# An attention and GEGLU block on one core: q of the plain units given out sooner, sums of squares on TensorE, one more buffer for exponentials

## The chip, the cores and the metric

The kernel runs on one core of one Trainium2 chip. The metric is the device time of one execution in microseconds (us). Before the change it is 1726.62 us at the median of three runs.

## The reference

```python
h = layernorm(x) * (1 + ca) + sa                 # x: 2048 x 512; ca, sa, ... from silu(c) @ w_mod
q = h @ wq                                       # 32 heads of 128
p = softmax(q @ k.T * 128 ** -0.5)               # k, v: 8 heads, the last 512 keys of the cache
x = x + ga * ((p @ v) @ wo)
h = layernorm(x) * (1 + cb) + sb
x = x + gb * ((gelu(h @ w_gate) * (h @ w_up)) @ w_down)   # 1792 wide
```

All inputs and the output are float32.

## The kernel before

**Products.** Almost every float32 product is three float16 products of 512 columns, high x high and the two mixed terms; `mm3` issues them (line 91, whose rows in the profile carry the names of their tiles). This text calls such a triple a group. The operands are scaled so that the halves fit; each scale comes from a sum of squares of a weight tile. `sumsq` takes it: a Square on ScalarE with `accum_out` over a tile of 128x512 (line 220). Then `sums` adds over partitions by a product with ones (line 224, tile `pst`), and `norm2` takes the root on GpSimd.

**Units and slots.** The attention is cut into 128 units: one head, 512 query rows, 512 keys. Each unit is four slots of 128 query rows, so there are 512 slots. In slot t TensorE makes the scores (`scores`, one group, tile `ps`, two buffers), VectorE the maximum (`peak`, line 1000), ScalarE the exponential (`expo`, line 1009, tile `ee`); ScalarE writes the scaled high half of slot t-2 (`high`, line 1021), VectorE the low half of slot t-3 (`low`, line 1026), and SP then issues the transpose of that tile into `pt` (line 1030). After the scores, TensorE takes up to three groups from a queue `work`, and when that is empty from `ywork`; in slots 0 to 7 it takes 2, 2, 0, 0, 2, 2, 0, 0.

**What lies in the queue.** At the first slot of unit u, `pushes` appends the groups that belong there: four groups that make q of the next unit (tile `pq`), four groups of probabilities times V for unit u-2 (tile `po`), and from unit 10 on parts of the next q by a seven-product scheme (tiles `qa`, `qb`, `qc`). The first twelve units, of weight groups g = 0, 1 and 2, are "plain": their q come from `q_plain`, four groups each, with both halves of wq in two tiles `rw`. Products with wo (tile `py`, four groups for 128 rows) come in `ywork` in units 7 to 11, and later in `work`, one such tile in a unit. The order of instructions on every engine is that of the program.

**Loads.** `sched` gives each load positions: the first is the slot of its first use, and the load goes out up to three slots ahead, when the buffer's last step lies behind it. `sched_pair` loads the two wq tiles of a weight group into two buffers `rw` and runs the square of each, then `w_spread`, then the splitting into halves; for group 1 GpSimd does the splitting (lines 161, 162, 165). All loads and transposes stand in SP's one queue.

**Places of the exponentials.** `expo` writes to SBUF (tag "e", 6 buffers), and for the slots named in `PSE` to a bank of PSUM, of the ring "acc" (5 banks, shared with `pq`, `po`, `py` and `pst`) or to the bank "qa".

Of the kernel before, what the change touches and what calls it, by code (L numbers as in the profile page):

```python
# [10 lines left out]
F32 = mybir.dt.float32  # L11
# [39 lines left out]
NP16 = 4  # L51
NV16 = 2
NPT = 3
NE = 6
CB = (11, 27)
PSE = dict.fromkeys((5, 7, 8, 9, 14, 18, 19, 21, 22, 23, 25, 26, 27), "acc") | dict.fromkeys((11, 15, 20, 24, 28), "qa")
EARLY = (2, 2, 0, 0, 2, 2, 0, 0)
WOS = ((6, 7, 8, 9), (-9, -8, -6, -5), (-16, -15, -14, -13))
WOP = ((23, 24, 26, 27), (10, 12, 16, 17), (-6, -4, 10, 12), (-6, -4, -3, -2))
# [6 lines left out]
def block_kernel(ctx: ExitStack, tc: tile.TileContext, x, kT, v, wq, wo, wg, wu, wd, cT, wc, wm, out):  # L66
# [141 lines left out]
    def mod_scale(j, name, const_, m=None, mid=nop, box=None):  # L208
# [6 lines left out]
        ts(cols[:, j:j + 2, :], cols[:, j:j + 2, :], inv, TOP13 / RT)  # L215
        pool_ts(col(name), s, const_ * RT / TOP13)

    def sumsq(out, src):
        with nc.allow_low_precision(reason="only a scale follows from it, which the margin in norm2 covers"):
            nc.scalar.activation(junk, src, AF.Square, scale=PRE, accum_out=out)  # L220

# [343 lines left out]
        return load, norm, split, turn  # L565

    def turned_out(qb, dt):
        tag, n = (("qt", 3), ("v16", 2))[dt % 2]
        f = pool.tile([P, D], F32, tag=tag, name="hf", bufs=n)
        v = f.rearrange("p (t q) -> p t q", t=QT)  # L570
        sc = cols[:, 4, dt:dt + 1]
        nc.scalar.activation(v, TURN[qb][:, :, dt, :], AF.Identity, scale=sc, bias=cols[:, 3, dt:dt + 1])
        put_off(2, lambda: nc.vector.scalar_tensor_tensor(v, TURN[qb][:, :, KT + dt, :], sc, v, op0=ALU.mult, op1=ALU.add))
        put_off(4, lambda: dma(spilled(3, qb)[:, dt, :], f))
# [57 lines left out]
        return pair("v16", "v16", 2)  # L632

    def get_qt():
        return pair("qt", "qt", 3)

    def get_w(k):
        return pair(f"w{k}", f"w{k}", 2)
# [106 lines left out]
    def at(key, *fns):  # L745
        later.setdefault(key, []).extend(fns)
# [488 lines left out]
    for g in range(NG):  # L1235
        half, pr = divmod(g, NPR)
        t0 = 16 * g
        qd = pr // 2
        srcs = [wq[2 * pr], wq[2 * pr + 1]]
        by = col("wsc", pr)  # L1240
        spread = None if half else lambda m, pr=pr: w_spread(pr, m)
        if 0 < g < GW:
            a, b = plain_steps(g, by)
            sched_pair(g, srcs, t0 - (19 if g > 1 else 13), spread, [(t0 - (12 if g > 1 else 8), a)], [(t0 - (8 if g > 1 else 7), b)])
        elif g >= GW and (not half or pr < GW):
            sched_set(g, srcs, t0, by, spread)
            if not half:
                a, b, c, d, e, f = SETPOS2 if g == GW else SETPOS
                for k, pos in ((0, t0 - b + 4), (3, t0 - c + 4), (1, t0 - e + 4), (2, t0 - f + 4)):
                    at(pos, lambda g=g, k=k: store_set(g, k))  # L1250
        elif half:
            for k, hi in ((0, 15), (1, 10), (2, 9), (3, 7)):
                within(t0 - 18, t0 - hi, lambda g=g, pr=pr, k=k: set_fetch(g, pr, k))
        if half:
            within(t0 - 14, t0 - 5, lambda pr=pr: k_fetch(pr))
            if pr % 2 == 0:
                within(t0 - 6, t0 + 3, lambda qd=qd: v_fetch(qd))
                for k in range(4):
                    within(t0 + 4 + 2 * k, t0 + 22 + 2 * k, lambda h=4 * qd + k: wo_fetch(h))
        else:  # L1260
            if g > 0:
                if pr % 2 == 0:
                    load, stat, spread_, parts = k_items(pr)
                    sched(t0 - (22 if g > 2 else 20), (load, [stat]))
                    at(("w", t0 - (19 if g > 2 else 17)), spread_)
                load, stat, spread_, parts = k_items(pr)
                sched(t0 - (7 if g > 2 else 4 if g > 1 else 6), (load, [parts if g != 2 else lambda parts=parts: soon(parts(True))]))
                at(t0 - (3 if g > 2 else 1 if g > 1 else 2), lambda pr=pr: store(("k", pr), KV[0, pr, 0]))
                if pr % 2 == 0:
                    load, stat, spread_, parts = v_items(qd)  # L1270
                    sched(t0 + 1, (load, [stat, spread_, parts]), t0 + 3, t0 + (6 if g > 2 else 5))
                    at(t0 + 10, lambda qd=qd: store(("v", qd), KV[0, qd, 1]))
            if pr % 2 == 0:
                wo_items(qd, [t0 + o + (qd == 7) for o in WOS[min(qd, 2)]], [t0 + o for o in WOP[min(qd, 2) + qd // 6]])
# [276 lines left out]
    def pushes(u, y):  # L1551
        g, k = divmod(u, 4)
        pv = pv_tasks(u - 2) if 2 <= u < NU + 2 else []
        if u >= NU:
            if k == 0:
                f = items(g)
                return y + f[4] + f[5] + pv + f[3]
            if k == 1:
                f = items(g + 1)
                return f[1] + f[2] + pv + f[6]  # L1560
            return []
        nxt = items(g + 1) if g + 1 >= GW else None
        if g < GW:
            w = q_plain(u + 1) if 0 < u + 1 < 4 * GW else []
            if u + 1 == 4 * GW:
                return nxt[2] + nxt[6] + pv + nxt[7]
            return w + pv + (nxt[1] if nxt and k == 2 else [])
        f = items(g)
        if k == 0:
            return y[:3] + f[4] + y[3:] + pv  # L1570
        if k == 1:
            return f[5] + y + nxt[1] + pv
        if k == 2:
            return f[3] + nxt[2] + y + pv
        return nxt[6] + y + pv + nxt[7]

    ctx.enter_context(tc.manual_schedule(engines={mybir.EngineType.SP}))
    with tc.manual_schedule():
        begin()
        nexty, invs = [], {}  # L1580
        for t in range(T + TAIL):
            now[0] = t
            u, s = divmod(t, 4)
            if s == 0:
                y = nexty.pop(0) if nexty and GW * 4 <= u <= NU else []
                if u > 2 and u % 2 == 1 and u - 2 < NU:
                    nexty += push_y(u - 2)
                work += pushes(u, y)
            if s == 2 and (t >= T or u < GW * 4) and nexty:
                ywork += nexty.pop(0)  # L1590
                while t >= T and nexty:
                    ywork += nexty.pop(0)
            if t < T:
                scores(t)
            inv = invs.pop(t, nop)
            if t < T:
                peak(t)
            run(("e", t))
            inv()
            if 0 <= t - LLAG < T:  # L1600
                low(t - LLAG)
            run(("d", t))
            if t < T:
                expo(t)
                if t % 2:
                    invs[t + 1] = recips(t - 1)
            if 0 <= t - HLAG < T:
                high(t - HLAG)
            run(("x", t))
            if 4 <= t < 4 + KT:  # L1610
                gate_cols(t - 4)
            for _ in range(4 if t >= T else EARLY[t] if t < len(EARLY) else 3):
                pop()
            run(t)
            for q in pending.values():
                while q and q[0][0] <= t:
                    q.pop(0)[2]()
            run(("w", t))
            spare(t)
            moved[0] = 0  # L1620
            if t == T + 2:
                for k in range(1, len(hold), 2):
                    for step in zip(*hold[k:k + 2]):
                        for fn in step:
                            fn()
                hold.clear()
        while ywork or work or any(k[0] in "dex" for k in later if isinstance(k, tuple)):
            now[0] += 1
            run(("e", now[0]))
            run(("d", now[0]))  # L1630
            run(("x", now[0]))
            for _ in range(4):
                pop()
            run(now[0])
        run(now[0] + 1)
        run(now[0] + 2)
        run(now[0] + 3)
# [90 lines left out]
    def yt_turn(g, c, qb):  # L1728

        def split():  # L1730
            tag, bufs = (("qt", 3), ("v16", 2))[YR.get("n", 0) % 2]
            u = YR["u", c, qb] = pool.tile([P, 2, QB], U16, tag=tag, name="yu", bufs=bufs)
            nc.scalar.activation(u, YT[g, c, qb].bitcast(U16).rearrange("p (r h) -> p h r", h=2), AF.Copy)

        def turn():
            if ("t", qb) not in YR:
                YR["t", qb] = pool.tile([P, KT, 2 * QT, P], U16, tag="pt", name="yv", bufs=NPT)
            nc.sync.dma_start_transpose(YR["t", qb][:, c], YR.pop(("u", c, qb)).rearrange("p a b -> p (a b)"))

        split()  # L1740
        put_off(3, turn)
        YR["n"] = YR.get("n", 0) + 1
        if YR["n"] == 3 * QT:
            put_off(4, lambda: rows_in(g, 1, (("acc", 2 * QT),) * 2))
# [116 lines left out]
```

## Time and profile before

| what | value |
|---|---|
| median of three runs | 1726.62 us (1725.72 to 1727.48) |
| span of the profiled execution | 1724.3 us, first to last instruction |
| time around the span, against the median | 2.3 us |
| TensorE / VectorE / ScalarE / GpSimd busy | 1705.4 / 1424.2 / 1257.4 / 1088.1 us |
| granted TensorE clock, mean | 0.999 |
| DMA queue of SP | 341.30 MB, 85.3% of 16 engines |

The profiled execution is listed by its span; its own time lies within the runs' 1725.72 to 1727.48 us. Slot 0 begins at 23.11 us, slot 12 at 53.08, slot 28 at 88.06, slot 64 at 181.38. A row of the timeline gives start, length, engine, line, tile written and tiles read, and the count of merged instructions; what stands in brackets is the idle time ahead of it and what ended it. PE rows are products, PEld rows are loads of the stationary operand.

### The profile page before, as it was taken

The numbers are of one execution on the slowest core, as the hardware profiler recorded it, in microseconds if no ns is written. First come the engines' busy times: TensorE is split into PE (matmuls) and PEld (weight loads), VectorE is DVE, ScalarE is ACT, GpSimd is POOL, SyncE is SP. The second block draws the span as 40 slices with busy tenths as digits, with TensorE's granted clock in tenths as the row PEclk, the third lists the DMA queues.
The fourth block names the chain that finished last, engine by engine and source line by source line (L and its number), as shares of the span: only waits on it lengthen the run. The fifth ranks groups of instructions, "written<-read, shape, count | busy, mean of one in ns | idle before, by whom it ended". The sixth has DMA issues, their size and how long they took to land.

```text
span 1724.3 us, 26250 instructions
## 1 busy us (share of the span) xinstructions
PE 1705.4 (99%) x7961; PEld 780.0 (45%) x7961; DVE 1424.2 (83%) x2480; ACT 1257.4 (73%) x2823; POOL 1088.1 (63%) x1322
## 2 busy tenths in 40 slices
PE   7999999999999999999999999999999999999999
PEld 4344444444444444444444444444444444444444
DVE  8888888888888999888888888888896788676666
ACT  7988788888878877888778777788785354455442
POOL 3879777776788884655665755757760345735424
PEclk9999999999999999999999999999999999999999
DMA  7999999999999998999999999899997556365353
GB/s 242 222 207 214 214 217 205 226 202 227 213 217 236 201 212 181 212 211 225 216 220 222 211 227 206 198 236 212 222 232 162 164 144 195 121 165 174 99 158 102
DMA packets 693454, 343.51 MB, mean 199 GB/s; under 512 B 579136, under 2 KB 602688, under 8 KB 693312
## 3 DMA queue, kind: packets, MB, share of 16 engines
q1 hardware_dynamic: 693024, 341.30, 85.3%
q8 instruction: 63, 1.03, 0.3%
q14 instruction: 79, 0.65, 0.1%
q10 hardware_dynamic: 288, 0.52, 0.1%
HBM read 137.50 MB, written 63.70 MB: 117 GB/s over the span
## 4 chain that ended last, share of the span: by engine, by line
PE 92%; ACT 4%; DVE 2%; DMA 2%; issue 1%; SPq 0%; ACTq 0%; DVEq 0%
PE py L91 20%; PE po L91 18%; PE ps L91 17%; PE fa L91 8%; PE qa L91 8%; PE fc L91 4%; PE qc L91 4%; PE ya L91 4%; PE qb L91 2%; PE fb L91 2%; PE yc L91 2%; ACT ee L1009 1%; ACT p L1021 1%; PE yb L91 1%; DMA rw<-in_wq 1%
## 5 line engine op out<-in xcount | busy, mean ns | idle before, releaser
L1009 ACT ACTIVATE ee<-ps,nm 128x512 f32<-128x512 f32 x512 | 349.7, 683 | 185.3 <-DVE nm L1000 182.7
L1026 DVE SCALAR_TENSOR_TENSOR p<-ee,rr,p 128x512 f16<-128x512 f32 x512 | 454.4, 888 | 8.5 <-ACT p L1021 8.0
L1000 DVE TENSOR_REDUCE nm<-ps 128x1 f32<-128x512 f32 x512 | 350.1, 684 | 96.8 <-PE ps L91 94.9
L91 PE MATMUL ps<-k,qt 128*128 128x512 f16 x1536 | 414.7, 379 | 4.4 <-ACT ee L1009 3.3
L1021 ACT ACTIVATE p<-ee,rr 128x512 f16<-128x512 f32 x512 | 363.9, 711 | 16.5 <-DVE rr L1017 11.8
L91 PE MATMUL po<-pt,v 128*128 128x512 f16 x1536 | 372.9, 379 | 2.1 <-DMA pt<-p 0.8
L91 PE MATMUL py<-wo,ot 128*128 128x512 f16 x1536 | 371.3, 379 | 0.0
L91 PEld LDWEIGHTS <-w 128*128 128x128 f16 x2184 | 213.4, 98 | 259.6 <-issue 2.0
L91 PEld LDWEIGHTS <-v 128*128 128x128 f16 x1536 | 149.8, 98 | 184.6 <-issue 3.0
L91 PEld LDWEIGHTS <-ot 128*128 128x128 f16 x1536 | 150.3, 98 | 181.2
L91 PEld LDWEIGHTS <-qt 128*128 128x128 f16 x1536 | 145.7, 98 | 178.0 <-issue 6.0
L1337 POOL TENSOR_TENSOR fg<-fg 128x512 f32<-128x512 f32 x48 | 62.9, 1311 | 135.8 <-DVE fg L1311 133.0
L754 DVE SCALAR_TENSOR_TENSOR ot<-po,ot 128x512 f16<-128x512 f32 x128 | 87.8, 686 | 40.4 <-ACT ot L753 39.9
L1321 ACT ACTIVATE at<-fg 128x512 f16<-128x512 f32 x92 | 56.3, 626 | 77.8 <-DVE fg L1311 61.0
L1009 ACT ACTIVATION_READ_ACCUMULATOR ee<-ps,nm 128x1 f32 x512 | 100.1, 196 | 0.0
L970 DVE SCALAR_TENSOR_TENSOR acc<-py,ysc,acc 128x512 f32<-128x512 f32 x128 | 94.7, 739 | 5.3 <-PE py L91 5.3
L91 PE MATMUL qa<-t,w 128*128 128x512 f16 x348 | 84.9, 379 | 0.0
L91 PE MATMUL fa<-t,w 128*128 128x512 f16 x336 | 81.7, 379 | 0.1
L237 POOL TENSOR_TENSOR lw<-lw,half__86 128x1 f32<-128x1 f32 x38 | 25.9, 681 | 85.7 <-DVE lw L188 85.6
L753 ACT ACTIVATE ot<-po 128x512 f16<-128x512 f32 x128 | 73.9, 578 | 5.0 <-PE po L91 5.0
L404 POOL TENSOR_TENSOR rs<-rs,nhalf 128x1 f32<-128x1 f32 x32 | 18.5, 577 | 93.7 <-DVE rs L398 85.8
L91 PEld LDWEIGHTS <-wo 128*128 128x128 f16 x504 | 49.3, 98 | 59.7 <-issue 0.5
(258 smaller groups left out, 2802.9 us busy)
## 6 DMA issues: line engine op xcount, KB each, us to landing
w<-kept SPq DMA_DIRECT2D x123, 256.0 KB, 3.3
wo<-kept SPq DMA_DIRECT2D x72, 256.0 KB, 3.2
kept<-stage SPq DMA_DIRECT2D x67, 256.0 KB, 3.0
raw<-in_wo SPq DMA_DIRECT2D x56, 256.0 KB, 3.2
kept<-w SPq DMA_DIRECT2D x39, 256.0 KB, 3.0
rw<-in_wq SPq DMA_DIRECT2D x38, 256.0 KB, 3.1
hs<-hf SPq DMA_DIRECT2D x32, 256.0 KB, 2.9
pt<-p SPq DMA_TRANSPOSE x512, 3.4
```

The lines of the kernel that those rows point to most:

```text
L91: nc.tensor.matmul(ps, a, b, start=first and n == 0, stop=last and n == 2, skip_group_check=chain)
L237: nc.gpsimd.tensor_tensor(out, out, half_, op=ALU.pow)
L404: nc.gpsimd.tensor_tensor(st["rs"], st["rs"], nhalf, op=ALU.pow)
L753: nc.scalar.activation(t[:, 0, :], src, AF.Copy, scale=scale)
L754: return lambda: nc.vector.scalar_tensor_tensor(t[:, 1, :], src, scale, t[:, 0, :], op0=ALU.mult, op1=ALU.subtract)
L970: nc.vector.scalar_tensor_tensor(acc[ti], st["p"], by, acc[ti], op0=ALU.mult, op1=ALU.add)
L1000: nc.vector.tensor_reduce(nm, E[t]["ps"], axis=AX.X, op=ALU.max, negate=True)
L1009: nc.scalar.activation(e, E[t]["ps"], AF.Exp, bias=E[t]["nm"], scale=1.0, accum_out=sm[:, t % 2:t % 2 + 1])
L1021: nc.scalar.activation(p16[:, 0, :], E[t]["e"], AF.Copy, scale=E[t]["r"])
L1026: nc.vector.scalar_tensor_tensor(p16[:, 1, :], E[t]["e"], E[t]["r"], p16[:, 0, :], op0=ALU.mult, op1=ALU.subtract)
L1321: nc.scalar.activation(t[:, 0, :], g, AF.Copy)
L1337: nc.gpsimd.tensor_tensor(g[o], g[a], g[b], op=ALU.subtract)
```

## The change

Four things change.

- `sumsq` in slots 0 to 27 calls the new `gram`: four float32 products of a tile's 128x128 parts with themselves, summed in a bank of "acc", and one read of its diagonal on VectorE with `accum_out`. 13 squares fall there: wq of groups 1 and 2 (4), K of group 2 (1), wo (8).
- `pushes` hands out q of units 5 to 11 by the table `QAT`, up to two units sooner; the tiles `qt` have five buffers in place of three. In units 8 to 11 a second tile of products with wo is put into `ywork` at the unit's first slot.
- The loads and squares of wq of group 2 start three slots sooner, its splitting three and five; the square of K of group 2 three slots sooner.
- `NE` is 7, and eight exponentials (slots 5, 7, 8, 19, 21, 23, 25, 27) go to SBUF and no longer to "acc".

```diff
-NE = 6
+NE = 7
+NQT = 5
+QAT = ((1,), (2,), (3,), (4, 5), (6, 7), (8,), (9, 10), (11,))
+GRAM = 28
-PSE = dict.fromkeys((5, 7, 8, 9, 14, 18, 19, 21, 22, 23, 25, 26, 27), "acc") | ...
+PSE = dict.fromkeys((9, 14, 18, 22, 26), "acc") | ...
...
+    def gram(out, src):
+        ps = bank("acc", "gram", NACC)
+        for k in range(KT):
+            sl = slice(k * P, (k + 1) * P)
+            nc.tensor.matmul(ps[:, 0:P], src[:, sl], src[:, sl], start=k == 0, stop=k == KT - 1)
+        ...
+            nc.vector.scalar_tensor_tensor(small.tile([P, P], F32, tag="gd", name="gd", bufs=1), ps[:, 0:P], PRE * PRE, ident, op0=ALU.mult, op1=ALU.mult, accum_out=out)
+
     def sumsq(out, src):
+        if 0 <= now[0] < GRAM:
+            return gram(out, src)
...
-            sched_pair(g, srcs, t0 - (19 if g > 1 else 13), spread, [(t0 - (12 if g > 1 else 8), a)], [(t0 - (8 if g > 1 else 7), b)])
+            sched_pair(g, srcs, t0 - (22 if g > 1 else 13), spread, [(t0 - (15 if g > 1 else 8), a)], [(t0 - (13 if g > 1 else 7), b)])
...
-                    sched(t0 - (22 if g > 2 else 20), (load, [stat]))
-                    at(("w", t0 - (19 if g > 2 else 17)), spread_)
+                    sched(t0 - (22 if g > 2 else 23), (load, [stat]))
+                    at(("w", t0 - (19 if g > 2 else 20)), spread_)
...
-            w = q_plain(u + 1) if 0 < u + 1 < 4 * GW else []
+            w = [q_plain(n) for n in (QAT[u] if u < len(QAT) else ())]
...
-            return w + pv + (nxt[1] if nxt and k == 2 else [])
+            return (w[0] if w else []) + pv + (w[1] if len(w) > 1 else []) + (nxt[1] if nxt and k == 2 else [])
...
-            if s == 2 and (t >= T or u < GW * 4) and nexty:
+            if (s == 2 and (t >= T or u < GW * 4) or s == 0 and u in (8, 9, 10, 11)) and nexty:
```

What this does to the order of instructions is shown at three places.

First, TensorE at the end of slot 10 (`po` is probabilities times V, `ps` the scores, `qt` the q halves, `pq` the next q, `w_659` and `w_691` the split wq). Before, the last product with V and the scores of slots 11 and 12, then the first product of the next q:

```order
L91 MATMUL po<-pt,v_588 128x512
L91 LDWEIGHTS qt
L91 MATMUL ps<-k,qt 128x512
...
L91 LDWEIGHTS w_659
L91 MATMUL pq<-b_201,w_659 128x512
```

Now, at the same place:

```order
L94 MATMUL po<-pt,v_600 128x512
L225 MATMUL gram<-rw 128x128 x4
L94 LDWEIGHTS qt
L94 MATMUL ps<-k,qt 128x512
...
L225 MATMUL gram<-rw 128x128 x4
...
L94 LDWEIGHTS w_691
L94 MATMUL pq<-b_201,w_691 128x512
```

The products on the two wq tiles of group 2 stand ahead of the scores of slot 11 and of slot 12.

Second, SP's queue in slots 6 to 11. `p_...` are probabilities by slot: `p_585`, `p_621`, `p_644`, `p_675` and `p_711` before, and `p_597`, `p_641`, `p_670`, `p_707` and `p_757` now, are those of slots 4 to 8. Before:

```order
L97 DMA wor<-in_wo 128x512
L1030 DMA_TRANSPOSE pt<-p_585 128x8x128
L97 DMA raw<-in_kT 128x512
L1030 DMA_TRANSPOSE pt<-p_621 128x8x128
L1030 DMA_TRANSPOSE pt<-p_644 128x8x128
L97 DMA u_689<-hs_1_473 128x512
L97 DMA raw<-in_kT 128x512
L1030 DMA_TRANSPOSE pt<-p_675 128x8x128
L97 DMA cb<-hs_1_473 128x512
L97 DMA rw<-in_wq 128x512
L1030 DMA_TRANSPOSE pt<-p_711 128x8x128
L97 DMA rw<-in_wq 128x512
```

Now:

```order
L100 DMA wor<-in_wo 128x512
L100 DMA raw<-in_kT 128x512
L1043 DMA_TRANSPOSE pt<-p_597 128x8x128
L100 DMA raw<-in_kT 128x512
L1043 DMA_TRANSPOSE pt<-p_641 128x8x128
L1043 DMA_TRANSPOSE pt<-p_670 128x8x128
L100 DMA u_721<-hs_1_473 128x512
L100 DMA rw<-in_wq 128x512
L1043 DMA_TRANSPOSE pt<-p_707 128x8x128
L100 DMA cb<-hs_1_473 128x512
L100 DMA rw<-in_wq 128x512
L1043 DMA_TRANSPOSE pt<-p_757 128x8x128
```

Each load of `rw` moves up by one transpose, while its first reader moves up by three slots; the loads of K move up by one transpose as well.

Third, TensorE at slot 32 (`py` is the product with wo). Before, after the scores of that slot:

```order
L91 MATMUL py<-wo,ot 128x512
L91 LDWEIGHTS qt
L91 MATMUL ps<-k,qt 128x512
...
L91 LDWEIGHTS w_1118
L91 MATMUL pq<-b_201,w_1118 128x512
```

Now:

```order
L94 MATMUL py<-wo,ot 128x512
L94 LDWEIGHTS qt
L94 MATMUL ps<-k,qt 128x512
...
L94 LDWEIGHTS v_600
L94 MATMUL po<-pt,v_600 128x512
```

The two or three groups of q that stood between the scores and the product with V are gone from here and from slots 36 and 40; they now stand in slots 14 to 27. Counted in groups, slots 14, 15, 18, 19, 26 and 27 gain 12, and slots 51, 54, 55, 58, 59, 62 and 63, which held products with wo, lose 12 as those are used up earlier.

More of the change, by code (lines that the diff above doesn't have):

```diff
@@ L53 @@
 NPT = 3
-NE = 6
+NE = 7
+NQT = 5
+QAT = ((1,), (2,), (3,), (4, 5), (6, 7), (8,), (9, 10), (11,))
+GRAM = 28
 CB = (11, 27)
-PSE = dict.fromkeys((5, 7, 8, 9, 14, 18, 19, 21, 22, 23, 25, 26, 27), "acc") | dict.fromkeys((11, 15, 20, 24, 28), "qa")
+PSE = dict.fromkeys((9, 14, 18, 22, 26), "acc") | dict.fromkeys((11, 15, 20, 24, 28), "qa")
 EARLY = (2, 2, 0, 0, 2, 2, 0, 0)
@@ L216, in mod_scale @@
         pool_ts(col(name), s, const_ * RT / TOP13)
+    def gram(out, src):
[3 more added lines that the diff above has]
+            nc.tensor.matmul(ps[:, 0:P], src[:, sl], src[:, sl], start=k == 0, stop=k == KT - 1)
+        with nc.allow_low_precision(reason="only a scale follows from it, which the margin in norm2 covers"):
+            nc.vector.scalar_tensor_tensor(small.tile([P, P], F32, tag="gd", name="gd", bufs=1), ps[:, 0:P], PRE * PRE, ident, op0=ALU.mult, op1=ALU.mult, accum_out=out)
     def sumsq(out, src):
+        if 0 <= now[0] < GRAM:
+            return gram(out, src)
         with nc.allow_low_precision(reason="only a scale follows from it, which the margin in norm2 covers"):
@@ L567, in turned_out @@
     def turned_out(qb, dt):
-        tag, n = (("qt", 3), ("v16", 2))[dt % 2]
+        tag, n = (("qt", NQT), ("v16", 2))[dt % 2]
         f = pool.tile([P, D], F32, tag=tag, name="hf", bufs=n)
@@ L634, in get_qt @@
     def get_qt():
-        return pair("qt", "qt", 3)
+        return pair("qt", "qt", NQT)
     def get_w(k):
@@ L1730, in split @@
         def split():
-            tag, bufs = (("qt", 3), ("v16", 2))[YR.get("n", 0) % 2]
+            tag, bufs = (("qt", NQT), ("v16", 2))[YR.get("n", 0) % 2]
             u = YR["u", c, qb] = pool.tile([P, 2, QB], U16, tag=tag, name="yu", bufs=bufs)
```

## The prediction

> **What bounds the kernel now.** I read the page first, then the busy time by stage, then TensorE's timeline in the first 100 us, then the queue of transfers.
>
> ```profile
> span 1724.3 us, 26250 instructions
> ...
> PE 1705.4 (99%) x7961; PEld 780.0 (45%) x7961; DVE 1424.2 (83%) x2480; ACT 1257.4 (73%) x2823; POOL 1088.1 (63%) x1322
> ```
>
> The profiled span is 1724.3 us; the runs took 1725.72 to 1727.48, so some 2.3 us lie around it at the median of 1726.62. I make the sum against the span and add it to the median. A share of 99% for TensorE says nothing on single stages, so here are those the change touches: slots 3 to 11, 12 to 27, 28 to 31, 32 to 51 and 52 to 63 (their edges are starts of scores). Columns: length, then busy us of PE, PEld, DVE, ACT, POOL, then the granted clock.
>
> ```profile
> 33.13:53.08 19.95, 17.87 (x75) 7.62 (x73) 16.25 (x31) 18.75 (x47) 15.09 (x23) 1.00 0.97 230
> 53.08:88.06 34.98, 32.42 (x147) 13.88 (x147) 29.18 (x58) 32.86 (x80) 28.21 (x38) 1.00 1.07 220
> 88.06:99.64 11.58, 10.70 (x49) 4.62 (x49) 10.13 (x20) 11.19 (x29) 6.81 (x11) 1.00 0.97 186
> 99.64:151.54 51.90, 51.90 (x245) 23.60 (x244) 45.41 (x81) 41.89 (x99) 44.87 (x55) 1.00 0.95 213
> 151.54:181.38 29.84, 29.84 (x141) 13.54 (x140) 25.86 (x45) 24.71 (x58) 26.75 (x33) 1.00 1.05 223
> ```
>
> Up to about 97 us ScalarE sets the pace (94% busy in both of the first rows) and TensorE has gaps; from 99.64 on TensorE has none. A product's busy time includes a tail that overlaps the next one, so I count gaps by the pace from start to start:
>
> ```profile
> 88.90 2.10 PE L91 MATMUL pq<-b,w 128*128 128x512 f16 x9
> 90.84 0.81 PE L91 MATMUL ps<-k,qt 128*128 128x512 f16 x3
> ```
>
> Nine products take 1.94 us, 0.2156 each, and a group of three 0.647. Slots 3 to 11 hold 9 scores and 12 groups (63 products, 13.6 us) and four gate products (3.4, below): 17.0 of 19.95, so 2.9 us of gaps. Slots 12 to 27: 144 products, 31.0 of 34.98, 3.9 of gaps. Slots 28 to 31: 48 products, 10.4 of 11.58, 1.2. In all 8.0 us. Since TensorE is full from there on, the end moves by what is added to TensorE's work, less the gaps that vanish, plus new gaps. That is the whole sum.
>
> **The products that replace the squares.** 13 squares fall into slots 0 to 27 (4 of wq, 1 of K, 8 of wo). Each becomes four float32 products of 128x128x128. The nearest rows:
>
> ```profile
> 5.58 3.47 PE L1041 MATMUL mps<-silu,wct 128*128 128x1 f32 x16
> ...
> 31.72 1.58 PE L443 MATMUL pln<-ident,xb 128*128 128x128 f32 x13
> ...
> 34.45 1.02 PE L1181 MATMUL gps<-wmr,silu 128*128 128x512 f32 x2
> 35.31 1.57 PE L91 MATMUL pq<-y,w 128*128 128x512 f16 x6
> ```
>
> A gate product (one instruction, two rows) keeps TensorE 0.86 us for 512 columns, four times a float16 product. For 128 columns that is 0.215, per square 0.86, for 13 squares **+11.2**. The transposes, 0.12 each, would give 6.3; the one-column products of the cold start, 0.217 a row and two rows each, 22.6. I take 11.2: it is the same kind of product in the same stage. None of it is hidden, but for the gaps counted next.
>
> On ScalarE the squares go, 0.61 us each on the chain:
>
> ```profile
> 39.90 0.61 ACT junk L220 x2
> ```
>
> That is 7.9 us off the engine which bounds slots 3 to 27. After the change TensorE needs more than ScalarE there (slots 12 to 27: 31.0 + 4 x 0.86 + 12 moved groups x 0.647 = 42.2 us against ScalarE's 32.86), so the relief is worth the gaps alone: at most **-8.0**, I take **-7.2**, since some waits have other causes; the low end is -5. The eight exponentials that go to SBUF, the diagonal's read on VectorE (13 times, between nothing and the 0.69 us of a 512-column read below, so 0 to 9 us beside 45.4 busy in 54.9 us) and the seventh buffer cost nothing while TensorE is the longer; without that cover VectorE would be full.
>
> ```profile
> L754 DVE SCALAR_TENSOR_TENSOR ot<-po,ot 128x512 f16<-128x512 f32 x9 | 6.2, 688 | 0.8 <-ACT ot L753 0.7
> ```
>
> **The wait that the earlier statistics add.** The statistics of the second wq pair (unit group 2) move from slots 13 and 14 to 10 and 11. Their buffers are two, held by group 1 until GpSimd has split it, and the loads stand in SP's queue behind the transposes of slots 6 and 7:
>
> ```profile
> 45.94 0.81 PE L91 MATMUL ps<-k,qt 128*128 128x512 f16 x3
> ...
> 49.04 0.81 PE L91 MATMUL ps<-k,qt 128*128 128x512 f16 x3
> ...
> 50.98 0.81 PE L91 MATMUL ps<-k,qt 128*128 128x512 f16 x3
> 53.08 0.81 PE L91 MATMUL ps<-k,qt 128*128 128x512 f16 x3 [1.29 <-ACT ee L1009]
> ```
>
> ```profile
> 48.32 2.61 SPq L1030 DMA_TRANSPOSE pt<-p  x2
> ...
> 55.27 0.39 SPq L97 DMA_DIRECT2D rw<-in_wq  x1
> ...
> 57.13 0.52 SPq L97 DMA_DIRECT2D rw<-in_wq  x1
> ```
>
> ```profile
> 50.11 1.16 POOL L162 TENSOR_TENSOR w<-rw,w 128x512 f16<-128x512 f32 x1
> ```
>
> ```profile
> 63.25 0.63 ACT L220 ACTIVATE junk<-rw 128x512 f16<-128x512 f32 x1 [0.69 <-DMA rw<-in_wq]
> ```
>
> ```profile
> DMA to landing us min/median/max: 3.1/4.6/7.0
> ```
>
> Before, the loads went out at 55.27 and 57.13, and even three slots later ScalarE still waited 0.69 us for the second. Now the reader is TensorE, in order, with the scores of slots 11 and 12 behind it, for which VectorE's maximum (queued behind the read of the diagonal) and ScalarE's exponential then wait. Slots 9, 10, 11 and 12 started at 45.94, 49.04, 50.98 and 53.08. Seven squares (6.0 us) less 1.4 us of gaps bring TensorE to the first of the two tiles at 50.98 + 4.6 = 55.6. Slot 9 starts about 3.4 later (five squares less 0.9 of gaps); the transpose of slot 6 ended 5.0 after that start (48.32 + 2.61 against 45.94), so now at 54.3, and the load follows at 54.4. GpSimd freed the buffer at 51.27 and is not later than that queue. Landing 4.6 on is 59.0: a wait of 3.4. The second load goes out about 59.0 and lands at 63.6; TensorE is there at 59.0 + 0.86 + 0.65 = 60.5: a wait of 3.1. With a discount for a shorter lag of ScalarE I take **+6.0**; ends 0 (loads out early) and 9 (7.0 us to land). K's statistic moves from slot 12 to 9 with its load one transpose ahead in SP's queue; that load goes out three slots before its reader, so I put nothing, at most 1.
>
> **The moved q.** Twelve groups (7.8 us) leave slots 51 to 63 for slots 14 to 27; TensorE's work stays the same, and the splits of three q on ScalarE and VectorE move under the same cover as the squares' relief. But in slots 52 to 63 it keeps 29.84 - 10 x 0.647 = 23.4 us, below ScalarE's 24.71; VectorE loses 2.5 additions of 0.74 and keeps 24.0. At the 94% that ScalarE reached when it bound, these slots take 26.3: **+2.9** of new gaps. Ends: 1.3 (ScalarE at 100%) and 4.5 (GpSimd's 26.75 as well).
>
> ```profile
> L970 DVE SCALAR_TENSOR_TENSOR acc<-py,ysc,acc 128x512 f32<-128x512 f32 x128 | 94.7, 739 | 5.3 <-PE py L91 5.3
> ```
>
> In slots 32, 36 and 40 no q stands ahead of the product with V any more, so it comes 1.3 us sooner after the transposed probabilities:
>
> ```profile
> 94.44 0.81 PE L91 MATMUL ps<-k,qt 128*128 128x512 f16 x3
> ...
> 104.85 0.81 PE L91 MATMUL ps<-k,qt 128*128 128x512 f16 x3
> ...
> 110.06 0.81 PE L91 MATMUL ps<-k,qt 128*128 128x512 f16 x3
> ```
>
> ```profile
> 98.50 1.23 SPq L1030 DMA_TRANSPOSE pt<-p  x1
> ...
> 107.84 1.23 SPq L1030 DMA_TRANSPOSE pt<-p  x1
> ```
>
> ```profile
> pt<-p SPq DMA_TRANSPOSE x13, 3.4
> ```
>
> Slot 34 starts at 104.85, its transpose goes out at 107.84 and lands 3.4 later, at 111.24; slot 36 has its scores done at 110.06 + 0.65 = 110.71. A wait of 0.5, three times: **+1.6**. Ends: 0, and 4.8 (slot 30's transpose went out 4.06 after 94.44, 1.6 too late).
>
> Sum: 11.2 - 7.2 + 6.0 + 2.9 + 1.6 = **+14.5**, so 1741 us.
>
> **Rules against the trace.** TensorE's clock fell once:
>
> ```profile
> 13.00:16.00 3.00, 0.81 (x5) 0.46 (x6) 2.02 (x10) 2.44 (x7) 0.19 (x1) 1.00 1.06 395
> 16.00:20.00 4.00, 4.00 (x12) 1.26 (x11) 3.69 (x14) 3.70 (x6) 2.36 (x3) 0.57 0.34 128
> ```
>
> After three us with 0.81 us of work the granted clock averaged 0.57 over four, which cost 4 x 0.43 = 1.7 us. Two waits of 3 us are like that stretch, so the same may come once or twice. The Trainium skill (TensorE: Matmul & The Clock Gate, "HAM oscillation") puts the limit at an idle window of about 3.4 us; the trace agrees with it, and by it the sum would be 16.2 to 17.9.
>
> The weights of a float32 product take longer to load than those of a float16 one, yet the 0.2156 pace shows no load at all:
>
> ```profile
> L91 PEld LDWEIGHTS <-w 128*128 128x128 f16 x120 | 11.6, 98 | 15.7 <-issue 1.5 <-DVE w L1071 0.6 <-DVE p L1026 0.5
> L443 PEld LDWEIGHTS pln<-ident,xb 128*128 128x128 f32 x16 | 1.9, 140 | 1.3 <-ACT xb L427 0.8 <-DVE xb L415 0.2
> ```
>
> If loads were exposed in the 104 short rows, 104 x 0.14 = 14.6 us would come on top. The Trainium skill (the same page, "The mechanism") says that a load overlaps a running product only where the row group differs, which would expose them; at 512 columns the trace disagrees.
>
> **Rivals.**
> - The loads are there in time and the new gaps are small: 11.2 - 8.0 + 1.3 + 1 = +5.5, 1732. Against it: the 63.25 row. Chance 0.2.
> - A clock fall on top: +16.2 to +17.9, 1743 to 1744.5. 0.12.
> - Loads of weights exposed: +29, 1756. 0.04.
> - The change does to the end nothing that can be measured (under 3.4 us, 0.2%, about what a measurement of this kernel can tell): 11.2 - 8.0, every gap filled and none new, +3.2. 0.08.
> - Faster: float32 products at float16's pace, 0.054 for 128 columns, cost 2.8 for all; with every gap filled and no wait, 2.8 - 8.0 = -5.2, 1721. It decides below 0.35 us a square. Against it: the gate's 0.86. 0.04.
>
> The forecast has 0.52, its own range 1735 to 1748. The range 1731 to 1750 takes in the loads in time and the upper ends of two terms; slower 0.90, same 0.06 (part of that case lies above the bound), faster 0.04.
>
> **What would show it.** Right: four short products a square at 0.2 us each; TensorE waiting for rw before 65 us, twice some 3 us; slot 28 starting some 18 us later than 88.06; gaps again where slots 52 to 63 lie; nothing changed behind. Wrong: squares at a quarter of the price, no wait for rw, or slots 52 to 63 without gaps.

## The result, and the profile after

The changed kernel takes 1750.58 us at the median of four runs (1750.48 to 1751.04) against 1726.63 before: a ratio of 1.0139, interval 1.0126 to 1.0152, so 24.0 us more. That is slower, as forecast, but 9.6 us above the predicted 1741 and 0.6 us outside the range. The profiled execution took 1750.66 us, with a span of 1748.9; 1.8 us lie around it.

The head of the page after. TensorE has 104 matmul instructions more and some 15 us more of busy time:

```profile
span 1748.9 us, 26445 instructions
...
PE 1720.3 (98%) x8065; PEld 793.8 (45%) x8065; DVE 1428.9 (82%) x2506; ACT 1251.8 (72%) x2797; POOL 1088.2 (62%) x1322
```

The same five stages as in the prediction (slots 3 to 11, 12 to 27, 28 to 31, 32 to 51, 52 to 63), cut at the new starts of scores. Columns: length, then busy us of PE, PEld, DVE, ACT, POOL, then the granted clock:

```profile
32.55:62.94 30.39, 27.21 (x148) 17.15 (x146) 20.02 (x50) 17.85 (x40) 18.89 (x26) 0.94 0.80 199
62.94:105.63 42.69, 42.65 (x218) 21.54 (x215) 33.91 (x69) 33.03 (x74) 31.04 (x37) 1.00 0.80 165
105.63:116.01 10.38, 10.38 (x51) 4.72 (x49) 8.26 (x17) 7.98 (x20) 3.08 (x7) 1.00 0.93 203
116.01:170.60 54.59, 51.44 (x240) 22.79 (x238) 43.80 (x80) 40.54 (x98) 44.31 (x55) 1.00 0.84 183
170.60:204.59 33.99, 27.09 (x112) 11.33 (x111) 25.49 (x42) 23.62 (x56) 25.83 (x33) 0.90 0.89 204
```

Against the lengths before, the five stages differ by +10.4, +7.7, -1.2, +2.7 and +4.2 us, 23.8 in all (slot 0 now starts 0.6 us earlier, at 22.52; shifts of slots are counted from slot 0). From slot 64 to slot 400 the shift grows by 0.1 us more, and at the last slot by 1.2, within the 2 us by which executions differ. Put by the same stages, the terms of the prediction give 11.1 (nine squares 7.7, gaps -2.6, the wait 6.0), 7.7 (four squares 3.4, moved groups 7.8, gaps -3.5), -1.1, 0.3 (1.6 less two groups that leave slot 51) and -3.6 (2.9 less ten groups). So the first three stages came within 0.7 us; the fourth is 2.4 off and the last 7.8. The last row shows where that lies: in slots 52 to 63 TensorE was busy for 27.09 us out of 33.99, at a mean clock of 0.90, where it has 23.4 us of work.

TensorE's timeline at the places that answer to the prediction (start, length, engine, line, tile written and tiles read; in brackets the idle time ahead and what ended it):

```profile
54.01 1.46 PE L94 MATMUL po<-pt,v 128*128 128x512 f16 x6
57.78 2.05 PE L225 MATMUL gram<-rw 128*128 128x128 f32 x8 [2.32 <-DMA rw<-in_wq]
59.62 1.49 PE L94 MATMUL ps<-k,qt 128*128 128x512 f16 x3
...
171.25 1.46 PE L94 MATMUL qc<-t,w 128*128 128x512 f16 x6
175.85 0.82 PE L94 MATMUL qa<-b,w 128*128 128x512 f16 x3 [3.15 <-POOL w L165]
...
178.51 2.43 PE L94 MATMUL po<-pt,v 128*128 128x512 f16 x6
...
191.82 1.46 PE L94 MATMUL qa<-t,w 128*128 128x512 f16 x6
197.03 1.00 PE L94 MATMUL po<-pt,v 128*128 128x512 f16 x3 [3.76 <-DMA pt<-p]
```

Three waits stand out: for a wq tile at slot 10, for GpSimd's split weights in slot 52, and for a transpose in slot 60. Behind each the next products take longer than such products do elsewhere: six with V take 2.43 us at 178.51 and 1.46 at 54.01. The clock behind the three waits, in stretches of 3.5 us, with the half us before the first:

```profile
57.00:57.50 0.50, 0.00 (x0) 0.00 (x0) 0.00 (x0) 0.00 (x0) 0.29 (x1) 1.00 0.10 37
57.50:61.00 3.50, 3.22 (x11) 2.11 (x11) 0.30 (x2) 0.00 (x0) 0.00 (x0) 0.51 0.87 209
177.00:180.50 3.50, 3.50 (x10) 1.25 (x9) 2.18 (x3) 2.26 (x6) 3.17 (x4) 0.51 0.43 125
197.50:201.00 3.50, 3.50 (x10) 1.29 (x9) 2.19 (x3) 2.29 (x7) 3.33 (x3) 0.51 1.03 257
```

Each wait was followed by 3.5 us at about half clock, which costs 1.7 us. The waits in slots 52 and 60 with a fall of the clock each make 10.3 of the 10.6 us by which slots 52 to 63 exceed TensorE's work (3.15 + 3.76 + 2 x 1.7).

### The profile page after: what moved, and what is told of

It reads as the page before. It is cut to its first block, busy times and chain, and to the rows that moved or that the text cites. A ratio compares the mean times of both kernels' runs of the same rounds, so it can differ in the third digit from the quotient of the medians.

```text
span 1748.9 us, 26445 instructions
## 1 busy us (share of the span) xinstructions
PE 1720.3 (98%) x8065; PEld 793.8 (45%) x8065; DVE 1428.9 (82%) x2506; ACT 1251.8 (72%) x2797; POOL 1088.2 (62%) x1322
## 4 chain that ended last, share of the span: by engine, by line
PE 89%; DVE 4%; ACT 3%; DMA 2%; POOL 1%; issue 1%; SPq 0%; POOLq 0%; DVEq 0%; ACTq 0%
PE py L94 18%; PE ps L94 17%; PE po L94 17%; PE fa L94 8%; PE qa L94 8%; PE fc L94 4%; PE qc L94 4%; PE ya L94 3%; PE qb L94 2%; PE fb L94 2%; PE yc L94 2%; PE pq L94 1%; PE yb L94 1%; DMA pt<-p 1%; DVE p L1039 1%
```

## The experiments

T1 in this section, Theory 1 in the expectations, is the theory read from this trace: the products cost what was forecast, and the q given out sooner costs three times its forecast, since slots 52 to 63 lack work for TensorE. Each kernel was timed in three rounds (the last in five) against the kernel before, whose median then was between 1727.0 and 1727.5; each difference is against that. A profiled execution can lie up to 2 us from its kernel's median, so differences of a few us between kernels rest on their slot starts as well.

**Squares on ScalarE again, everything else as changed.**

```diff
-GRAM = 28
+GRAM = 0
```

> All sums of squares go back to ScalarE; q sooner, the earlier statistics and the buffers stay as in the changed kernel (1750.6; before 1726.6). Theory 1 (the loss has two halves: 11.6 us of float32 products with the waits at slots 10 and 11, and an emptied queue in slots 51 to 63, where TensorE meets work that GpSimd and the transposes have not finished, each wait with a stretch of half clock behind it): the second half stays, and slots 12 to 27 get longer since ScalarE now has the squares and three more q: 1738 (1734 to 1742). Theory 2 (nearly all of the loss hangs on the float32 products; q sooner costs nothing or gains): 1727 or below.

Measured: 1740.87 against 1727.47, ratio 1.0076 (1.0061 to 1.0091), +13.4. The rival, that the products cause the loss, would have given no loss. TensorE's waits in the first 215 us (in all, times, longest) show the same two places without a single float32 product of a square:

```profile
PE po L94 <- DMA pt<-p: 5.8, 3, 3.3
PE ps L94 <- ACT ee L1022: 3.6, 3, 2.1
PE qa L94 <- POOL w L165: 3.2, 1, 3.2
```

So more than half of the loss comes without the products. By slot 12 only 0.5 us are lost here, in place of 10.4; the rest comes behind it, where the moved q stands.

**q handed out as before, products and early statistics kept.**

```diff
-            w = [q_plain(n) for n in (QAT[u] if u < len(QAT) else ())]
+            w = [q_plain(u + 1)] if 0 < u + 1 < 4 * GW else []
...
-            if (s == 2 and (t >= T or u < GW * 4) or s == 0 and u in (8, 9, 10, 11)) and nexty:
+            if s == 2 and (t >= T or u < GW * 4) and nexty:
```

> q and the products with wo are given out as before; the float32 products and the earlier statistics stay. Theory 1: slots 3 to 11 still cost 10.4, slots 12 to 31 about -1, slots 32 to 63 as before, with no wait for GpSimd near slot 52 and none for a transpose near slot 60: 1736 (1734 to 1739). Theory 2: the loss stays, 1745 or more.

Measured: 1738.29, ratio 1.0064 (1.0047 to 1.008), +10.8. Slot 12 starts 10.4 us late, as in the changed kernel; slot 28 is 13.0 late, slot 32 11.8, and from there to slot 68 the shift stays at 11.8. Neither the wait at slot 52 nor that at slot 60 is there. (Slots 12 to 31 lost 1.4 us where the theory had them win 1.) So without the moved q nothing is lost in slots 32 to 63, and some 13 us are its price (24.0 - 10.8 by the medians). By the slot starts of the two traces it is 12.0: 5.1 in slots 12 to 27, 2.7 in slots 32 to 51 and 4.2 in slots 52 to 63.

**The second wq pair's squares on ScalarE.**

```diff
-        if 0 <= now[0] < GRAM:
+        if 0 <= now[0] < GRAM and now[0] not in (10, 11):
```

> Of the changed kernel only the two squares of the second wq pair (slots 10 and 11) go back to ScalarE, so that TensorE no longer waits for these loads. Theory 1: 1.8 us of products, 3.5 of waits and 1.7 of half clock go, some 2 come back because ScalarE waits for the same loads: 1745.5 (1743 to 1748). Theory 2 (the wait is only shifted, the exponentials behind ScalarE's square hold the scores instead): 1749, by the 1.8 us of products alone.

Measured: 1744.8, ratio 1.0095 (1.008 to 1.011). Slot 12 is 3.5 us late instead of 10.4. Of the 7.0 us that slot 12 gains by taking TensorE out of the wait for these two tiles, 6.4 are left at slot 64 (6.6 by the medians; the 7.0 are two squares, 1.8, and the wait with its fall of the clock, 5.2).

**GpSimd's wo splits out of the way of slot 52.** GpSimd's timeline after, ahead of the split `w` that slot 52 waits for:

```profile
167.96 1.27 POOL L676 TENSOR_TENSOR raw<-raw,gs 128x512 f32<-128x512 f32 x1
...
172.66 1.20 POOL L168 TENSOR_SCALAR rw<-rw,wsc 128x512 f32<-128x512 f32 x1
...
174.64 1.15 POOL L165 TENSOR_TENSOR w<-rw,w 128x512 f16<-128x512 f32 x1
```

The first row belongs to the splitting of a tile of wo, the others to that of the weights; the split ends at 175.79, 5.2 us after slot 52 starts. Before it ended 4.6 us after that, so GpSimd is hardly later. But then four groups with wo stood in slots 52 and 53 ahead of the first `qa`, which began in slot 54, 5.8 us after slot 52; they are gone, and `qa` is due in slot 52 itself, at 1.9 us. The edit moves two splits of wo by three slots, behind the weights (`WOP` holds the slots):

```diff
-WOP = (..., (10, 12, 16, 17), ...)
+WOP = (..., (10, 12, 19, 20), ...)
```

> Of the changed kernel only GpSimd's order changes: two wo tiles are split three slots later, so that the weights of group 4 are ready sooner. Theory 1: the wait of 3.3 us at slot 52 and the 1.7 us of half clock behind it go, the wait for a transpose at slot 60 stays: 1745.5 (1744 to 1748). Theory 2 (GpSimd is full there, or VectorE and ScalarE set the pace of these slots): the time is lost again a few slots later, 1750.

Measured: 1750.8, ratio 1.0133 (1.0118 to 1.0148), no gain. T1's number fell and the rival held: the wait in slot 52 shrank from 3.15 to 0.7 us, but slots 60 and 61 took 8.6 us more than before, against 5.6 in the changed kernel; 1.0 of it is a wait for another of GpSimd's splits. The chain of waits there (start, length, what):

```profile
189.36 1.15 POOL wo L165
...
191.18 1.47 POOL w L165
...
192.73 0.24 POOL ysc L254
192.97 0.04 SPq L100
...
193.06 0.03 SPq L1043
...
193.11 5.66 DMA pt<-p
198.77 0.05 issue
198.82 1.46 PE po L94 x3
```

The wo splits now end at 190.5, another weight split and a scale come after them, SP's load of `rw` waits for its buffer, and the transpose queued behind that load goes out with it and takes 5.66 us to land. Behind this wait the granted clock was 0.50 for 6.8 us, in place of 3.4, which adds 1.7 us; the same came at slot 10, which the edit does not touch. GpSimd has work that must be done somewhere in this stage; moved from in front of one wait it stands in front of the next.

**The wait kept, the clock kept up.** Thirteen float16 products on idle data, into a free bank, ahead of the third group in slots 52 and 60, where TensorE waits anyway:

```diff
+                if n_ == 2 and t in (52, 60):
+                    fps = bank("acc", "fill", NACC)
+                    for _ in range(13):
+                        nc.tensor.matmul(fps, junk[:, 0:P], junk, start=True, stop=True)
```

> The changed kernel (1750.6) with 13 empty float16 products (2.8 us, on a bank of their own) put in front of the two products that wait longest, at slots 52 and 60, so that TensorE works through most of each wait. Theory 1 (an idle stretch of some 3 us is followed by a stretch at half clock, 1.7 us lost each time): the waits end at the same moments, the half clock behind them goes, 1747.2 (1746 to 1749). Rival (the slow products behind the waits have another cause, or the clock falls anyway): 1750.6 or more.

Measured: 1748.06, ratio 1.0123 (1.0108 to 1.0139). The stage itself gained 3.5 us (it is 0.6 us longer than before instead of 4.2). Slot 64 is only 1.5 us sooner than in the changed kernel, since slot 14 came 1.9 us later here, in a stage that the edit does not touch: behind the wait at slot 10 the clock was at half for twice as long, 6.8 us, which is 1.7 us more:

```profile
59.10:66.00 6.90, 5.48 (x18) 2.91 (x17) 3.33 (x10) 1.61 (x5) 0.00 (x0) 0.51 0.46 111
```

TensorE's timeline at the two places:

```profile
175.23 2.98 PE L1629 MATMUL fill<-junk 128*128 128x512 f16 x13 [0.52 <-ACT junk L233]
178.04 0.81 PE L94 MATMUL qa<-b,w 128*128 128x512 f16 x3
...
193.61 2.97 PE L1629 MATMUL fill<-junk 128*128 128x512 f16 x13
197.17 0.82 PE L94 MATMUL po<-pt,v 128*128 128x512 f16 x3 [0.59 <-DMA pt<-p]
198.47 2.11 PE L94 MATMUL po<-pt,v 128*128 128x512 f16 x9
```

Nine products with V take 2.11 us again. So the half clock at these two places was 3.5 us, 1.7 to 1.8 each, and it follows from the idle time, since work in the same stretch keeps it away.

**Products on the bfloat16 upper halves.** They read the upper 16 bits of each number, with the same count of products.

```diff
+        b = src.bitcast(BF16).rearrange("p (n h) -> p n h", h=2)
...
-            nc.tensor.matmul(ps[:, 0:P], src[:, sl], src[:, sl], start=k == 0, stop=k == KT - 1)
+            nc.tensor.matmul(ps[:, 0:P], b[:, sl, 1], b[:, sl, 1], start=k == 0, stop=k == KT - 1)
```

> The changed kernel with each float32 product replaced by one bfloat16 product of the upper 16 bits of the same values (only the sums of squares lose digits). Theory 1 (the products lie on TensorE's path nearly all the way, but TensorE then reaches the late wq loads sooner): 13 x 0.67 = 8.7 us of products go, 3 to 4 of them turn into longer waits at slots 10 and 11: 1745.5 (1742 to 1748); the limit is 1740.9, the time without any such product. Rival (what comes later sets the time, the products are hidden): 1750.

Measured: 1744.52, ratio 1.0102 (1.0087 to 1.0117). TensorE comes sooner to the wq tiles and waits for them instead:

```profile
55.79 0.41 PE L226 MATMUL gram<-rw 128*128 128x128 bf16 x4 [4.57 <-DMA rw<-in_wq]
56.03 1.02 PE L94 MATMUL ps<-k,qt 128*128 128x512 f16 x3
```

A square takes 0.24 us from start to start instead of 0.89, but the wait grew from 2.3 to 4.6 us. Of the 8.5 us that thirteen cheaper squares are worth, 3.7 are left at slot 28 (14.4 us late instead of 18.2): the wait took 2.3, and the clock behind it, at half for 6.8 us in place of 3.4, another 1.7.

**Each square's products issued twice.**

```diff
-        for k in range(KT):
+        for k in [*range(KT), *range(KT)]:
...
```

> The changed kernel with each sum of squares taken twice over by its products: eight float32 products in place of four (the value doubles, so the scales differ). Theory 1: 13 x 0.89 = 11.6 us more on TensorE's path, little of it hidden, since slots 12 to 27 are full and the loads at slots 10 and 11 shift along: 1761.5 (1759 to 1764). Rival (half of it is taken up by the waits at slots 10, 11 and 52 to 60): 1756.

Measured: 1759.34, ratio 1.0188 (1.0171 to 1.0205). Slot 28 is 12.1 us later than after the change: 0.93 us a square, all of it on the path. Of these 12.1, 2.6 are taken back up to slot 64, nearly all in slots 52 to 63: the wait in slot 60 is 2.0 us instead of 3.8, with no fall of the clock behind it. The end lies at the lower edge of the theory's range, 2.2 us below its number.

**Only the wo products back at their old slots, q still sooner.**

```diff
-            if (s == 2 and (t >= T or u < GW * 4) or s == 0 and u in (8, 9, 10, 11)) and nexty:
+            if s == 2 and (t >= T or u < GW * 4) and nexty:
```

> q sooner as in the changed kernel, but the products with wo are given out as before, so the 12 groups are missing in slots 33 to 43 and no longer in 51 to 63. Theory 1a (the place matters: at slots 52 and 60 TensorE meets GpSimd's weights and the transposes, at 33 to 43 there is more room): the 10 us of gaps in slots 52 to 63 go, some 3 come back in slots 33 to 43: 1743.5 (1741 to 1746). Theory 1b (an emptied queue costs the same wherever it lies, because VectorE and ScalarE are nearly as full as TensorE): 1749 or more.

Measured: 1746.58, ratio 1.0114 (1.0099 to 1.0129), between the two: 0.6 us above the first theory's range, 2.4 below the second's number. Ten of the twelve missing groups are now missing in slots 33 to 43. The waits at slots 52 and 60 are gone: from slot 48 to 60 the shift stays at 21.4 us, and it is 21.2 at slot 64. In their place come two waits ahead of the products with V: 1.9 us at slot 36, which ends as a transpose lands (129.34 us), and one at slot 40:

```profile
PE po L94 <- POOL v L165: 4.1, 1, 4.1
```

The one at slot 40 was 1.8 us in the changed kernel, where the clock stayed up; here the granted clock was 0.50 behind it, at 142 to 144 us. So the products with wo had filled slots 32 to 47 in part; put there they are missing in slots 51 to 63, and put back they are missing at slots 36 and 40.

**Products alone.** q as before, and the statistics of group 2 at their old places too:

```diff
-            ... t0 - (22 if g > 1 else 13), spread, [(t0 - (15 if g > 1 else 8), a)], [(t0 - (13 if g > 1 else 7), b)])
+            ... t0 - (19 if g > 1 else 13), spread, [(t0 - (12 if g > 1 else 8), a)], [(t0 - (8 if g > 1 else 7), b)])
...
-                    sched(t0 - (22 if g > 2 else 23), (load, [stat]))
-                    at(("w", t0 - (19 if g > 2 else 20)), spread_)
+                    sched(t0 - (22 if g > 2 else 20), (load, [stat]))
+                    at(("w", t0 - (19 if g > 2 else 17)), spread_)
```

> The float32 products alone: q, the products with wo and the statistics of group 2 in the order of before (the squares of its wq pair at slots 13 and 14, three slots after their loads). Theory 1 (the price is 11.6 us of products less the gaps that they and the relieved ScalarE fill; the 4 us between this and the kernel with q given back at 1738.3 are the waits for wq at slots 10 and 11 and the half clock behind them): 1733 (1731 to 1736). Rival (TensorE waits for the same loads at slots 13 and 14): 1737.

Measured: 1732.39 against 1727.29, ratio 1.0032 (1.0019 to 1.0045), +5.1. No wait for a wq tile is left; K's tile costs one:

```profile
PE gram L225 <- DMA raw<-in_kT: 0.8, 1, 0.8
```

So the early statistics cost the other 5.7 us of the 10.8 (5.0 by the slot starts). The seventh buffer and the new places of the exponentials are in this kernel too, so they cost no more than its 5.1 us; no kernel takes them away alone.

**Bfloat16 products alone, ten of them** (not in slots 12, 13 and 14, where ScalarE squares):

```diff
+        b = src.bitcast(BF16).rearrange("p (n h) -> p n h", h=2)
...
-        if 0 <= now[0] < GRAM:
+        if 0 <= now[0] < GRAM and now[0] not in (12, 13, 14):
```

> A version meant to beat both: order of before, ten of the thirteen squares (not K and not the second wq pair) as bfloat16 products of the upper 16 bits, 2.2 us in all, which takes 6.1 us off ScalarE where ScalarE sets the pace. Theory 1 (gaps of 8.0 us in slots 3 to 31 are there because of ScalarE, and some of them go): 1724 (1722 to 1726.5). Rival (the gaps have other causes, VectorE and the transposes, and nothing is won beyond the products' own 2.2 us): 1727 to 1729.

Measured: 1726.10 against 1727.29, ratio 0.9993 (0.9984 to 1.0002): no gain that can be measured, though the time lies in the first theory's range. Slot 30 starts 1.1 us sooner than before, slot 36 only 0.15. The waits for transposes in the first 215 us (0.8 in all before):

```profile
PE po L94 <- DMA pt<-p: 1.6, 2, 1.1
```

The second of them, 0.54 us in slot 33, took back about half of the 1.0 us lost between slots 30 and 36: a TensorE that is sooner by a us reached the products with V before the transpose had landed. Where the rest went is not shown.

## Why the prediction was right or wrong

**The products, +11.2: right.** The row of one square, and the product behind it:

```profile
42.19 1.05 PE L225 MATMUL gram<-wor 128*128 128x128 f32 x8
43.08 0.17 PE L237 MATMUL pst<-lm,ones 128*128 128x2 bf16 x1
```

The 43.08 start is 0.89 us behind 42.19. The row counts two passes a product, so eight passes are one square of four products: 0.22 us a product, 0.89 a square, 11.6 for thirteen. Doubling them gave 0.93 a square. The nearest row, the gate's 0.86 for 512 columns, was the right one to divide by four. The rival of exposed weight loads (+29) is out, since 0.89 has no room for it, and so is that of a float16 pace. What the gaps gave back, -7.2, needs the moved q as well: with the products alone the loss is 5.1 us by the medians and 6.8 by slot starts (in an execution 1.9 us above its median), where 11.2 - 7.2 gives 4.0.

**The wait for the wq tiles, +6.0: right in size, another make-up.** Its price alone measured 5.7 by the medians and 5.0 by slot starts. The prediction had two waits of 3.4 and 3.1. The first was 2.3 us by its row, the second 0.86, and between them lay the fall of the clock, 1.7 us; 4.9 in all. The loads, on SP's queue:

```profile
53.75 0.40 SPq L100 DMA_DIRECT2D rw<-in_wq  x1
...
58.31 0.37 SPq L100 DMA_DIRECT2D rw<-in_wq  x1
```

```profile
rw<-in_wq SPq DMA_DIRECT2D x2, 256.0 KB, 3.7
```

```profile
61.97 1.13 PE L225 MATMUL gram<-rw 128*128 128x128 f32 x8 [0.86 <-DVE nm L1013]
```

They went out 0.7 us sooner than reckoned (54.4 and 59.0) and landed in 3.9 and 3.5 us where 4.6 was taken. The row of the second square names VectorE's maximum; the tile itself landed at 58.31 + 3.5 = 61.8, the same moment, so either may have been last. That the sum came out is luck in part: it was kept by a clock fall that the prediction held as a rival.

**The moved q: the term that failed.** It stood as +2.9 of new gaps in slots 52 to 63, on the reasoning that ScalarE at 94% would then set the pace, and +1.6 in slots 32 to 40. Measured, slots 52 to 63 have 10.6 us of gaps (33.99 - 23.4), 10.3 of them the two waits of 3.15 and 3.76 us with a fall of the clock behind each, and the loss in slots 32 to 51 is 2.4 us over its terms. The step that failed compared the busy sums of the engines (24.71, 24.0 and 26.75 us in a stage of 26 to 30). (Its upper end of 4.5 does not follow from these figures either: GpSimd's 26.75 less 23.4 is 3.4, and 5.1 at 94%.) No engine was over-full there, and TensorE still stopped where a product came sooner than what it reads: `qa` is due 1.9 us into slot 52 instead of 5.8, and GpSimd's split of its weights ended at 5.2 instead of 4.6. With the groups of wo put back into these slots, and q still sooner, both waits were gone. The size of the wait could have been read from the trace of before:

```profile
154.56 1.61 POOL L162 TENSOR_TENSOR w<-rw,w 128x512 f16<-128x512 f32 x1
```

```profile
157.37 0.81 PE L91 MATMUL qa<-b,w 128*128 128x512 f16 x3
```

The split ended at 156.17 and its first reader started at 157.37: 1.2 us of slack, for a product that now comes 3.9 us sooner (four groups with wo and the scores of two slots, six groups of 0.647). That gives 2.7; with the split 0.6 later it is 3.3, and 3.15 was measured. This sum was made with the result known. Of the groups that leave these slots the prediction used only the sum.

In slot 60 the wait was for a transpose. Its row on SP's queue and its landing in the chain of waits:

```profile
191.74 1.23 SPq L1043 DMA_TRANSPOSE pt<-p  x1
...
191.74 5.24 DMA pt<-p
```

It went out half a us after slot 60 began and landed 5.24 us on; the prediction had no wait there, and used the 3.4 us of the page before as the landing of all transposes, though in the trace of before single ones already took up to 6.5 us in the first 215 us. The three waits at slots 32, 36 and 40 were to be 0.5 each for transposes; the one at slot 32 is 0.49, at slot 36 there is none for a transpose, and at slot 40 TensorE waited 1.82 us for V's split on GpSimd, which the prediction had not in it:

```profile
117.32 2.10 PE L94 MATMUL po<-pt,v 128*128 128x512 f16 x9 [0.49 <-DMA pt<-p]
...
140.26 2.12 PE L94 MATMUL po<-pt,v 128*128 128x512 f16 x9 [1.82 <-POOL v L165]
```

**The clock.** The rival had one or two falls of 1.7 us at slots 10 and 11, on top of the sum. Three came, 5.1 us in all; one stood where the rival put it, the other two behind waits that the sum had no place for. The Trainium skill (TensorE: Matmul & The Clock Gate, "HAM oscillation") states the rule that no idle gap of TensorE be over about 3.4 us. As a limit on one idle stretch the traces do not bear it out: at slot 10 the last product ended at 55.47 and the clock was down at 57.6, 2.1 us later, while no product ran, and it stayed down for 3.4 us. The prediction took the trace of before to agree with it, but there the longest single gap ahead of the fall at 16.2 us was 1.19 us.

The traces fit another reading, found with all of them at hand. Within one trace the falls lie whole multiples of 3.41 us apart (after the change at 57.60, 177.06 and 197.54 us, 35 and 6 of them), so they stand on a fixed grid. Between 20 and 215 us of the ten traces with a fall in the first 215 us, the clock fell at the end of each of the 18 windows of this grid of which products covered less than 0.40, and of none of which they covered 0.43 or more. It stayed at half for a second window where they covered 0.79 or less of the first, and rose where it was 0.86 or more. So the same wait may cost its length alone or more, by where it falls on the grid: waits of 2.03 and 2.06 us in slot 60 (squares twice, and the second wq pair on ScalarE) had no fall behind them, one of 2.15 there with the bfloat16 products had.

**The rest.** VectorE's read of the diagonal, bounded at 0 to 9 us in all, took 0.29 us each, thirteen times, and was hidden:

```profile
L227 DVE SCALAR_TENSOR_TENSOR gd<-gram,ident x13: 275/291/292, 36.3 to 105.8; 128x128 f32<-128x128 f32 x13
```

Next to nothing changed behind slot 64, as forecast.

What stays open: why the transpose at 191.74 took 5.24 us to land. SP issued loads of `rw` 0.6 us ahead of it and 1.3 us behind it; no kernel here took those loads away. Between 25 and 215 us of the twelve traces, 63 of the 504 transposes that went out within 1.5 us behind a load took over 4.5 us, and 7 of the 301 others; that goes with a queue of loads as the cause, and does not show it.

## What to carry to other kernels

When work is moved out of a stage in which the bounding engine has no gaps, compare, for each product that now comes sooner, the time it gains with the slack of what it reads, and not the busy sums alone: here 3.9 us against 1.2. Price a wait on TensorE with the fall of the clock that may stand behind it: here each of 2.3 us or more had one, none under 2.0 us had, and it cost 1.7 us, or 3.4 where TensorE was not busy again at once. And set what a moved operation costs the engine that takes it against the gaps which that engine has in that stage: thirteen squares were 11.6 us of TensorE against 8.0 us of gaps, and even ten cheap ones gave nothing that could be measured.

## What the runs showed of the hardware

- A float32 product of 128 columns takes 0.22 us, a quarter of the 0.86 us of one with 512, with no room in that for its weight load, so the load is hidden.
- The clock fell behind waits of 2.3, 3.2 and 3.8 us and was at half for 3.4 us each time (6.8 at five places in other kernels). The falls of a trace lie multiples of 3.41 us apart, and each stood at the end of such a window of which products covered less than 0.40. Empty products in the wait keep it up (3.5 us gained in two places).
- A transpose landed in 3.4 us at the median of the kernel before, and in 5.2 and 5.7 us at the two places where TensorE waited longest for one.
